# A new table of instruction order and engine choice for a fused cluster-attention and maxout-FFN kernel

## The chip, the cores and the metric

The kernel runs on one core of one Trainium2 chip. The metric is the device time of one execution in microseconds (us); lower is better. The core has five engines that work at the same time and wait for each other through semaphores: TensorE (PE in the profile; its weight loads are PEld), VectorE (DVE), ScalarE (ACT), GpSimd (POOL) and SyncE (SP), which here only issues DMAs.

## The reference

Attention in which a query sees only keys of its own cluster, then a feed-forward layer with a maximum of three products:

```python
# q, k, v: 4 x 8 x 768 x 64; centroids: 8 x 16 x 64; w1, w2, w3: 512 x 768; w_out: 768 x 512
q_assign = argmax(einsum('bhsd,hcd->bhsc', q_n, c_n)); k_assign = the same of k
scores = where(q_assign == k_assign, q @ k.T / sqrt(D), -1e9)
attn = exp(scores - max) / (sum + 1e-9)
x = (attn @ v), heads side by side: 3072 x 512
out = maximum(maximum(x @ w1, x @ w2), x @ w3) @ w_out
```

## The kernel before, in words

The work is cut into 3077 *units*, small closures that each issue one to a few dozen instructions on one engine. Nothing is scheduled at run time: `ORDER` is a written-out list of the 3077 unit numbers, and `Plan.run` calls the units in that order, so each engine's queue holds its own units in the order of the list and runs them strictly in turn. 1104 of the units are *flexible*: they may be issued on VectorE, ScalarE or GpSimd (some on the DMA queue). `HANDS` is a string with one letter for each of them, in the order of unit numbers: V, S, G or Q. Both tables come from a search over the planner's costs (the numbers in us in each `add`); at run time only the tables count.

The stages of the work are interleaved by the table:

- **Preparation of q and k** (`prep`, `mask_rows`, `first_rows`), 16 pairs of heads: load, scale by powers of two, split in a 16-bit high and low part (tile `qk`, lines L380, L378, L382, L804 to L818), cluster scores on TensorE, one-hot rows of the cluster (tile `cl_t`, L527 to L626).
- **Weights** (`weights`, `piece`, `split16`), all in the first 200 us: 24 pieces of 64-bit words are turned into float32 by a cast (tile `top`, L1024 on ScalarE, L1026 on GpSimd) and an integer instruction on VectorE (L1030, from `wd` and `top` to `wf`), then scaled and split (L1041 to L1046). The row maximum of a group is L1070.
- **192 score tiles** (`tile_units`), 48 for each of four batches: four matmuls into a PSUM tile `big` (L1256, L1258); a row maximum on VectorE (L1267, one for each tile, so its count is a ruler for progress); the exponential on ScalarE (L1273); the split in high and low part (`hi`: L378 on ScalarE, L382 on GpSimd or VectorE; `lo`: L1279 on GpSimd or VectorE); then a transposing DMA. 20 tiles of the first batch are transposed on TensorE instead (L1304) and split from PSUM into `pt` (high part L378 or L382, low part L1312 on VectorE). From the second batch on, rows are divided by their sum first (L1293, L1294, then L1321 or L1323, or within L380 and L1332).
- **24 visits** (`visit`), each after six tiles: 36 matmuls with v (L1207). In the first batch the division by the sums follows (L1199 spreads the reciprocals through TensorE, `spread` takes them out of PSUM into `xs` by L378 on ScalarE or L382 on VectorE, L1226 multiplies).
- **Feed-forward** (`ffn`), 8 blocks of 384 tokens: 18 groups of 12 matmuls each (L1413), their evictions with the running maximum (L1427, L380 or L382), a split (L987, L989, L1142), and three output groups of 18 matmuls (L1468) whose results are stored.

The PSUM buffers are few: three `big` and two `one`. A unit that needs a buffer waits for the last user of what lay there before:

```python
        for n in order:
            u = self.units[n]
            for x in u.leases:
                x()
            u.fn(u.hand) if u.pick else u.fn()
...
            for x in u.leases:
                x.left -= 1
                if not x.left:
                    self.places[x.tag].append(x.place)
```

`x()` takes the place that came free first, in the order of the list. So the list also sets which buffer a tile gets, and whose end it waits for.

Of the kernel before, what the change touches and what calls it, by code (L numbers as in the profile page):

```python
# [1534 lines left out]
```

## Time and profile before

| | |
|---|---|
| median of 3 runs | 710.59 us (707.4 to 712.21) |
| profiled execution, its own time | 711.06 us |
| its span, first to last instruction | 709.1 us |
| PE busy | 665.5 us (94%) |
| DVE busy | 599.0 us (84%) |
| ACT busy | 483.6 us (68%) |
| POOL busy | 403.3 us (57%) |
| mean granted TensorE clock | 0.978 |

The times are whole-device times. The span is 2 us shorter than the time of the same execution, since it begins at the first instruction and ends with the last. Busy shares are means over the whole span; the stages differ, so the stretches of the profile are to be read one by one.

### The profile page before, as it was taken

How to read it: one execution, taken by the hardware profiler on the slowest of the kernel's cores; microseconds unless marked ns; L12 is line 12 of the kernel's file. 1: busy time of each engine (PE TensorE's matmuls, PEld its weight loads, DVE VectorE, ACT ScalarE, POOL GpSimd, SP SyncE). 2: the span in 40 equal slices, each digit the busy share in tenths (PEclk: the TensorE clock that was granted, in tenths of full speed). 3: DMA queues.
4: the chain of work that ended last, by engine and by line, in shares of the span. 5: the costliest groups of instructions: out<-in, count | busy, mean ns of one | idle time of the engine just before them, and what ended most of it. 6: DMA issues, size and time to landing. Idle time of an engine off the chain costs nothing. (4 is left out here: it accounts for less than half of the span.)

```text
span 709.1 us, 13176 instructions
## 1 busy us (share of the span) xinstructions
PE 665.5 (94%) x4505; PEld 389.9 (55%) x4505; DVE 599.0 (84%) x1470; ACT 483.6 (68%) x841; POOL 403.3 (57%) x374
## 2 busy tenths in 40 slices
PE   3778778998999999999999999999999999999997
...
PEclk8578999999999999999999999999999999999999
...
GB/s 225 199 216 182 207 210 205 188 174 202 168 196 188 172 126 217 197 185 195 215 156 194 179 189 181 185 196 196 197 194 178 145 164 112 148 158 125 1 1 60
DMA packets 297795, 121.03 MB, mean 171 GB/s; under 512 B 273024, under 2 KB 284160, under 8 KB 297728
## 3 DMA queue, kind: packets, MB, share of 16 engines
...
## 5 line engine op out<-in xcount | busy, mean ns | idle before, releaser
L1267 DVE TENSOR_SCALAR_CACHE_REDUCE big<-big,nsc 128x768 f32<-128x768 f32 x192 | 192.7, 1016 | 11.4 <-PE big L1258 10.8
L1413 PE MATMUL one<-x,w16a 128*128 128x384 f16 x1152 | 197.0, 326 | 0.2
L1279 POOL TENSOR_TENSOR hl<-e,hl 128x768 f16<-128x768 f32 x86 | 144.4, 1682 | 61.1 <-ACT hl L378 34.2
L1413 PEld LDWEIGHTS <-w16a 128*128 128x128 f16 x1152 | 111.5, 98 | 75.7 <-issue 2.9
L1273 ACT ACTIVATE e<-big,nm 128x768 f32<-128x768 f32 x116 | 104.4, 901 | 49.7 <-DVE big L1267 32.3
L1256 PE MATMUL big<-qk 128*128 128x512 f16 (+1 forms) x384 | 96.6, 334 | 12.2 <-ACT e L1273 9.4
L1207 PE MATMUL big<-pt,v 128*64 128x384 f16 x1152 | 101.8, 330 | 2.4 <-ACT e L1273 1.4
L1413 PE MATMUL one<-x,w16b 128*128 128x384 f16 x576 | 98.9, 326 | 1.0 <-DVE worow L1098 1.0
L1258 PE MATMUL big<-qk 96*128 96x512 f16 (+1 forms) x384 | 96.1, 331 | 0.1
L1273 ACT ACTIVATE big<-big,nm 128x768 f32<-128x768 f32 x76 | 66.3, 872 | 43.7 <-DVE big L1267 35.3
L1207 PEld LDWEIGHTS <-v 128*64 128x64 f16 x1152 | 70.0, 111 | 33.2 <-issue 9.8
L1413 PEld LDWEIGHTS <-w16b 128*128 128x128 f16 x576 | 55.7, 98 | 40.1 <-issue 3.4
L1332 DVE SCALAR_TENSOR_TENSOR hl<-big,rs,hl 128x768 f16<-128x768 f32 x72 | 72.7, 1011 | 4.6 <-ACT hl L380 3.6
L380 ACT ACTIVATE hl<-big,rs 128x768 f16<-128x768 f32 x62 | 55.7, 898 | 27.3 <-issue 10.7
L1323 POOL TENSOR_SCALAR e<-e,rs 128x768 f32<-128x768 f32 x37 | 34.0, 919 | 65.9 <-DVE rs L1294 47.1
L1256 PEld LDWEIGHTS <-qk 128*128 128x128 f16 x384 | 35.3, 99 | 43.7 <-issue 22.1
L378 ACT CAST hl<-e 128x768 f16<-128x768 f32 x60 | 49.8, 831 | 5.3 <-POOL e L1323 4.5
L1258 PEld LDWEIGHTS <-qk 96*128 96x128 f16 x384 | 38.2, 100 | 27.1 <-issue 2.6
L818 POOL TENSOR_TENSOR qk<-stage,qk 128x768 f16<-128x768 f32 x26 | 43.8, 1686 | 9.2 <-ACT qk L378 5.5
L1468 PE MATMUL one<-wo,vf_h 128*128 128x512 f16 x216 | 48.3, 379 | 0.5 <-ACT o L380 0.4
L1468 PE MATMUL one<-wo,wf_h 128*128 128x512 f16 x216 | 48.3, 379 | 0.0
L1427 DVE SCALAR_TENSOR_TENSOR wf_h<-one,wf_h 128x384 f32<-128x384 f32 x48 | 26.5, 553 | 20.2 <-PE one L1413 19.6
...
## 6 DMA issues: line engine op xcount, KB each, us to landing
...
```

The lines of the kernel that those rows point to most:

```text
L378: eng.copy(out, x)
L380: eng.activation(out, x, AF.Copy, scale=k)
L818: eng.tensor_tensor(t()[:, AQ, i], x(), t()[:, BQ, i], op=ALU.subtract)
L1207: nc.tensor.matmul(t()[D * i : D * i + D, 0:nb], v()[:, i, kt, a], pts[i % len(pts)]()[:, rows[i], c * QT + kt, :], start=(m == 0), stop=( ...
L1256: nc.tensor.matmul(t()[:, lo:hi], aq[:, qs], ak[:, lo:hi], start=True, stop=False)
L1258: nc.tensor.matmul(t()[:, lo:hi], bq[0:K2, qs], bk[0:K2, lo:hi], start=False, stop=True)
L1267: nc.vector.tensor_scalar(s, s, -SCALE if exact else nscs[:, b, pr : pr + 1], 3.0e38, op0=ALU.mult, op1=ALU.min, accum_out=nm())
L1273: nc.scalar.activation(e(), t()[:, 0:S], AF.Exp, bias=nm(), scale=-1.0, accum_out=r)
L1279: eng.tensor_tensor(hl()[:, 1, :], e(), hl()[:, 0, :], op=ALU.subtract)
L1332: eng.scalar_tensor_tensor(hl()[:, 1, :], e(), r(), hl()[:, 0, :], op0=ALU.mult, op1=ALU.subtract)
L1413: nc.tensor.matmul(t()[:, 0:nb], w16[jt // JA][:, jt % JA, wa, i, ct], x16[b, gi, ct]()[:, xa, 0:nb], start=(m == 0), stop=(m == 3 * CT - 1),)
L1468: nc.tensor.matmul(t()[:, 0:DM], h16(jt)[:, ha, tt * P : (tt + 1) * P], wo16[0][:, jt, wa, :], start=(m == 0), stop=(m == 3 * JT - 1),)
```

## The change: other tables of order and of engines

`ORDER` and `HANDS` are replaced, nothing else. The unit closures, the planner's costs, the buffers and their counts are the same. 279 of the 1104 flexible units get another engine: 59 go from ScalarE to GpSimd, 55 from ScalarE to VectorE, 51 from VectorE to ScalarE, 45 from GpSimd to ScalarE, 36 from VectorE to GpSimd and 33 from GpSimd to VectorE. In instructions VectorE goes from 1280 to 1281, ScalarE from 626 to 608, GpSimd from 379 to 396; TensorE has 8651 and SyncE 374 in both.

```diff
 ORDER = """
-1 0 18 19 51 52 173 445 151 2-5 7 6 54 53 8-15 20 21 30 22-24 39 25 26 40 27 55 28 16 31 33 36 35 56 41 57 63
+1 0 19 18 51 52 151 173 2-5 7 6 53 54 8-15 21 20 30 22-24 39 25 55 26 40 27 56 29 28 41 16 33 31 36 174 57 63
...
 HANDS = """
-VVSSSSSSVVSSSSSSGSGSGGQQGVSSGSGSVGQQGVSSSSGSSGQQGVSGGSVGSSGSSGGSGVSSGSSGSSGSSGVGSGSSGVSGSGGVVSGSGGSGGGGGVSGGSS
+VVSSSSSVVVSSSSSSSSGSGGQQGVSSGGGSSGQQGSVSGGGSSVQQGVSGGGSGSSVSSGGSSVSSGGSGGSGSGSVGSGSSGVSGSSSVSSGSSGSGGSSGVVSGGS
...
```

**First place, TensorE some 50 us into the program.** L1304 transposes a finished tile, L412 spreads a scale of the weights, L1256 and L1258 are the next score tile, L1207 is the first product with v. Before:

```order
L1304 MATMUL big<-ident,e 128x128 x6
L412 LDWEIGHTS sc_m
L412 MATMUL one<-ident,sc_m 128x128
L1256 LDWEIGHTS qk
L1256 MATMUL big<-qk 128x512
L1256 LDWEIGHTS qk
L1256 MATMUL big<-qk 128x256
L1258 LDWEIGHTS qk
L1258 MATMUL big<-qk 128x512
L1258 LDWEIGHTS qk
L1258 MATMUL big<-qk 128x256
L1207 LDWEIGHTS v_326
```

The same place after:

```order
L412 LDWEIGHTS sc_m
L412 MATMUL one<-ident,sc_m 128x128
L1256 LDWEIGHTS qk
L1256 MATMUL big<-qk 128x512
L1256 LDWEIGHTS qk
L1256 MATMUL big<-qk 128x256
L1258 LDWEIGHTS qk
L1258 MATMUL big<-qk 128x512
L1258 LDWEIGHTS qk
L1258 MATMUL big<-qk 128x256
L1304 MATMUL big<-ident,e 128x128 x6
L1207 LDWEIGHTS v_412
```

The score tile now stands ahead of the transposes of an older tile, where it stood behind them.

**Second place, VectorE some 31 to 38 us into the program.** `hl`, `qk` and `v` are high parts, L543 and L555 belong to the one-hot rows, L733 is an absolute maximum of q and k. Before:

```order
L1267 TENSOR_SCALAR big,nm<-big,nsc 128x768
L382 TENSOR_SCALAR v_397<-vf 128x12x64
L757 SCALAR_TENSOR_TENSOR nsc<-q_p 128x1
L382 TENSOR_SCALAR hl<-e 128x768
L543 TENSOR_TENSOR cl_t_313<-rank,cl_m_314 128x768
L1267 TENSOR_SCALAR big,nm<-big,nsc 128x768
L1312 TENSOR_TENSOR pt<-big,pt 128x768
L1030 SCALAR_TENSOR_TENSOR wf<-wd,top 128x512
L382 TENSOR_SCALAR qk<-stage_261 128x768
L555 TENSOR_SCALAR cl_t_313<-one,ksel 128x768
L1312 TENSOR_TENSOR pt<-big,pt 128x768
L1267 TENSOR_SCALAR big,nm<-big,nsc 128x768
```

The same place after:

```order
L1030 SCALAR_TENSOR_TENSOR wf<-wd,top 128x512
L543 TENSOR_TENSOR cl_t_314<-rank,cl_m_315 128x768
L762 TENSOR_REDUCE q_s<-q_r 128x1
L1267 TENSOR_SCALAR big,nm<-big,nsc 128x768
L626 STREAM_TRANSPOSE cl_t_239<-onehot_99 128x768
L1267 TENSOR_SCALAR big,nm<-big,nsc 128x768
L1312 TENSOR_TENSOR pt<-big,pt 128x768
L733 TENSOR_REDUCE q_m_391<-stage_373 128x1
L382 TENSOR_SCALAR pt<-big 128x768
L1267 TENSOR_SCALAR big,nm<-big,nsc 128x768
L1312 TENSOR_TENSOR pt<-big,pt 128x768
```

Four eviction-sized steps have left VectorE here (`v`, `hl`, `qk`, L555, all to ScalarE), and two have come to it (L733 and a high part `pt` from PSUM, both from ScalarE).

**Third place, VectorE some 80 us into the program**, between two score tiles of the first batch. Before:

```order
L415 TENSOR_REDUCE wcol<-one 128x1
L416 RECIPROCAL sc_s<-wcol 128x1
L1030 SCALAR_TENSOR_TENSOR wf<-wd,top 128x512
L1267 TENSOR_SCALAR big,nm<-big,nsc 128x768
L1043 TENSOR_SCALAR wf<-wf,sc_s 128x512
L1030 SCALAR_TENSOR_TENSOR wf<-wd,top 128x512
L1312 TENSOR_TENSOR pt<-big,pt 128x768 x2
```

The same place after:

```order
L1267 TENSOR_SCALAR big,nm<-big,nsc 128x768
L1030 SCALAR_TENSOR_TENSOR wf<-wd,top 128x512
L1043 TENSOR_SCALAR wf<-wf,sc_s 128x512
L1267 TENSOR_SCALAR big,nm<-big,nsc 128x768
L1030 SCALAR_TENSOR_TENSOR wf<-wd,top 128x512
L1312 TENSOR_TENSOR pt<-big,pt 128x768
L382 TENSOR_SCALAR xs<-one 128x384
L1312 TENSOR_TENSOR pt<-big,pt 128x768
```

A `spread` (`xs` from PSUM) has come to VectorE from ScalarE; there are four such of eight in the new table and none in the old one.

## Rows read from the trace of the kernel before

**Rows 1.** The page, parts 1 and 2: busy time of each engine with its share and count, and the span in 40 slices of 17.7 us (tenths busy; PEclk is the granted TensorE clock in tenths).

```profile
span 709.1 us, 13176 instructions
PE 665.5 (94%) x4505; PEld 389.9 (55%) x4505; DVE 599.0 (84%) x1470; ACT 483.6 (68%) x841; POOL 403.3 (57%) x374
PE   3778778998999999999999999999999999999997
PEclk8578999999999999999999999999999999999999
```

**Rows 2.** Busy time of each engine in stretches of the span: the stretch, its length, then PE, PEld, DVE, ACT, POOL busy us (instructions), the granted clock, the DMA share and GB/s.

```profile
20.00:60.00 40.00, 33.30 (x187) 22.32 (x187) 36.48 (x76) 35.21 (x59) 29.49 (x21) 0.71 0.85 197
60.00:200.00 140.00, 121.71 (x912) 74.54 (x910) 136.37 (x311) 125.31 (x231) 111.93 (x100) 1.00 0.82 193
200.00:300.00 100.00, 99.45 (x677) 58.20 (x676) 87.03 (x225) 66.06 (x112) 57.87 (x49) 1.00 0.90 180
300.00:400.00 100.00, 99.74 (x691) 57.30 (x689) 93.17 (x244) 72.72 (x125) 65.99 (x55) 1.00 0.94 188
400.00:640.00 240.00, 239.31 (x1626) 139.00 (x1625) 209.52 (x532) 163.50 (x284) 128.40 (x111) 1.00 0.88 172
640.00:710.00 70.00, 65.20 (x399) 35.55 (x397) 20.95 (x39) 6.84 (x12) 2.76 (x4) 0.99 0.18 45
```

**Rows 3.** The end of the chain that ended last: start us, us, what.

```profile
...
655.29 3.05 PE big L1207 x36
658.34 35.21 PE one L1413 x216
693.54 11.67 PE one L1468 x54
```

**Rows 4.** Who waited for whom from 20 to 200 us, for TensorE and for VectorE: the waiting engine, tile and line, what ended the wait, us in total, times, the longest.

```profile
PE big L1256 <- ACT e L1273: 9.4, 12, 1.4
PE big L1304 <- ACT e L1273: 3.7, 5, 1.3
...
DVE big L1267 <- PE big L1258: 1.6, 4, 1.0
DVE xs L1226 <- PE big L1207: 1.5, 2, 1.3
```

**Rows 5.** VectorE in order of time at two places: some 53 to 59 us, and at 199.5 us the 57th row maximum. Columns: start us, us, engine, line, operation, operands, count, and in brackets the idle time before it and what ended it.

```profile
53.96 1.02 DVE L1267 TENSOR_SCALAR_CACHE_REDUCE big<-big,nsc 128x768 f32<-128x768 f32 x1 [0.99 <-PE big L1258]
58.66 0.56 DVE L1226 TENSOR_TENSOR xs<-big,xs 128x384 f32<-128x384 f32 x1 [1.28 <-PE big L1207]
199.51 1.01 DVE L1267 TENSOR_SCALAR_CACHE_REDUCE big<-big,nsc 128x768 f32<-128x768 f32 x1
```

**Rows 6.** VectorE's groups by line and shape: line, operation, out<-in with shapes, count, busy us, mean ns of one, idle us before.

```profile
L1312 DVE TENSOR_TENSOR pt<-big,pt 128x768 f16<-128x768 f32 x20 | 18.9, 950 | 1.2 <-ACT pt L378 0.9
L1279 DVE TENSOR_TENSOR hl<-e,hl 128x768 f16<-128x768 f32 x10 | 10.6, 1057 | 0.3
L382 DVE TENSOR_SCALAR hl<-big,rs 128x768 f16<-128x768 f32 x10 | 10.1, 1014 | 0.2
L382 DVE TENSOR_SCALAR hl<-e 128x768 f16<-128x768 f32 x13 | 7.2, 552 | 0.6 <-ACT e L1321 0.6
L382 DVE TENSOR_SCALAR wf_h<-one 128x384 f32<-128x384 f32 x13 | 7.2, 552 | 3.3 <-PE one L1413 3.2
L382 DVE TENSOR_SCALAR o<-one,so 128x512 f32<-128x512 f32 x8 | 6.0, 748 | 9.6 <-PE one L1468 9.6
L818 DVE TENSOR_TENSOR qk<-stage,qk 128x768 f16<-128x768 f32 x4 | 5.4, 1342 | 0.0
L382 DVE TENSOR_SCALAR qk<-stage 128x768 f16<-128x768 f32 x4 | 2.5, 628 | 0.0
L1323 DVE TENSOR_SCALAR e<-e,rs 128x768 f32<-128x768 f32 x4 | 3.3, 821 | 0.0
L989 DVE TENSOR_SCALAR vf_h<-vf_h 128x384 f16<-128x384 f32 x8 | 2.8, 354 | 0.0
L904 DVE TENSOR_TENSOR v<-stage,v 128x768 f16<-128x768 f32 x2 | 1.9, 951 | 0.0
L589 DVE TENSOR_TENSOR cl_t<-cl_t,cl_m 128x384 f32<-128x384 f32 x2 | 1.7, 859 | 0.0
```

**Rows 7.** TensorE from 49 to 59 us in order of time, the columns of rows 5.

```profile
49.35 0.48 PE L1256 MATMUL big<-qk 128*128 128x512 f16 x2 [1.13 <-ACT e L1273]
50.61 1.54 PE L1304 MATMUL big<-ident,e 128*128 128x128 f32 x6 [0.45 <-ACT e L1273]
52.44 0.84 PE L1256 MATMUL big<-qk 128*128 128x512 f16 x2
53.85 4.74 PE L1207 MATMUL big<-pt,v 128*64 128x384 f16 x36
```

**Rows 8.** The integer instruction L1030 on VectorE: its row by line (duration ns min/median/max, first and last start), one instance, and one of GpSimd at that place (start us, us).

```profile
L1030 DVE SCALAR_TENSOR_TENSOR wf<-wd,top x24: 672/692/1945, 19.8 to 156.3; 128x512 int32<-128x512 int32 x24
...
43.47 1.95 DVE L1030 SCALAR_TENSOR_TENSOR wf<-wd,top 128x512 int32<-128x512 int32 x1
...
43.22 1.64 POOL L1279 TENSOR_TENSOR hl<-e,hl 128x768 f16<-128x768 f32 x1
```

**Rows 9.** The group of the same line by shape: count, busy us, mean ns.

```profile
L1030 DVE SCALAR_TENSOR_TENSOR wf<-wd,top 128x512 int32<-128x512 int32 x24 | 19.2, 799 | 0.3 <-POOL w16a L1046 0.2 <-ACT top L1024 0.2
```

More of the change, by code (lines that the diff above doesn't have):

```diff
@@ L77 @@
-1507 1479 1470 1497 2699 1498 1508 1492 1483 1509 1460 2700 2702-2704 1510 1493 1461 1499 1511 1494 1462 1484
[7 rows of a table removed]
-1602 1618 1610 1603 1625 2729 601 633 1626 2730 1611 605-607 2733 1633 1642 2735 2731 1619 1627 1628 1634 1643
[8 rows of a table removed]
-1695 1723 1733 691 712 1741 2762 2763 619 1734 713 714 620 684 1742 2764 2768 1735-1737 1724 1725 695 621 1738
[12 rows of a table removed]
-1869 1870 2812 2946 1904 1839 1896 1871 1905 1872 1897 1873 1840 2814 1898-1900 1882 1891 1874 1912 2817 1913
-1914 2818 1906 1901 1929 2819 2821 1920 2815 1915 1916 1930 1917 1918 1907 1931-1933 1908 2816 2820 2822 1921
[10 rows of a table removed]
@@ L119 @@
-2071 2078 2859 2079 817 2091 2861 792 2092 818 819 2100 2080 820-822 2072 2860 793 2093 859 2862 2053 856 2064
[11 rows of a table removed]
-2900 893 2230 848 2231 2225 2237 2902 2245 918 913 914 2212-2214 877 2198 936 2215 2226 2905 2253 2907 2238
[11 rows of a table removed]
-945 2407 2396 3007 2367 2388 2950 2377 2368 2397 2408 2400-2402 3067 2409 2410 2952 2411 2415 2423 2424 2416
-2425 2954 2443 2412 2403 2417 2426 2404 2418 2419 2427 2413 2428 2420 2444 2445 2955 2378 2435 2379 2429 2421
-2380 2430 2446 2447 2436 2448 2437 2452 2957 2959 2469 2405 2422 2431 2414 2453 2438-2441 2470 2958 2471 2454
[9 rows of a table removed]
@@ L155 @@
-3010 3015 2596 3017 3019 3018 3020 3021 3025 3022-3024 3026 3027 3029 3028 3033 3030 3031 3034 3032 3035 3037
-3036 3041 3038-3040 3042 3043 3045 3044 3046-3049 3051 3050 3052 3053 3057 3054 3058 3055 3056 3059 3061 3060
-3062-3064 3068 3071 3069 3070 3016 3074 3072 3073 3075 3076
+1 0 19 18 51 52 151 173 2-5 7 6 53 54 8-15 21 20 30 22-24 39 25 55 26 40 27 56 29 28 41 16 33 31 36 174 57 63
[15 rows of a table added]
+1137 1149 1119 1143 1138 1150 229 1144 230-232 1120 1139 1151 1140 1116 245 248 1121 1141 1145 246 1146 247
[14 rows of a table added]
@@ new lines @@
+388 1273 1282 1252 492 1283 2635 1284 1288 389-393 494 495 2645 434 1248 421 432 525 431 465 1274 2637 439
[3 rows of a table added]
+1307 472 473 1314 2649 1315 1316 1256 502-504 1320 505 1326 1335 1321 1294 1322 1327 474 1336 475 2651 536
+1292 1308 1317 477-479 476 538 1328 1323 1337 1343 1295 1324 1338 1339 1329 506 532 1344 1340 1345 1296 533
+507 534 1297 1341 1298 1299 509 535 570 2650 1325 510 480 508 1355 1363 1346 512 1330 1356 1357 2652 1300
+1331-1333 1372 2657 2654 1373 1358 1359 1364 1360 2658 1374 537 513 514 1361 539 540 1347 1348 1365 2655 1349
[5 rows of a table added]
@@ new lines @@
+2765 1427 561 1412 1371 555 1388 556 628 1396 1405 583 2681 2683 2680 1428 2682 562-564 1429 1413 1414 1422
+488 2684 565 1430 1415 2685 2689 1443 1423 1424 489 2686 2766 1435 1444 2687 1431 1436 1445 1437 1438 1432
+1446 2691 1451 1406 1416 569 566-568 1425 1433 1447 1439 2688 1440 1452 1448 2690 1453 1407 1449 546 2692 1454
+1408 1455 1456 1441 1457 2693 1471 1463 1488 2697 1472 1464 1458 2694 577 1473 1465 1450 1442 1459 1474 1466
+1467 1475 2695 1476-1478 1489 1468 2698 1490 1480 2701 1505 1469 1506 1491 1492 1481 1507 1493 2696 2656 1470
@@ new lines @@
+1479 2653 584 1497 2699 1498 1460 1508 2700 1509 1482 1499 2702 2703 1510 2704 1483-1485 1500 1494 1511 1501
[5 rows of a table added]
+1591-1593 1597 599 1584 595 2723 2724 596 1585 1598 1605 2725 1613 1594 2827 1599 1606 1607 1614 597 1586 602
[8 rows of a table added]
+652 1702 1714 690 2757 1721 1676 2759 653-655 1691 1709 1710 2758 1715 1692 656 657 2755 1693 1716 658 1722
[18 rows of a table added]
+1953-1955 1967 1959 1968 1969 1960 1961 1974 1983 2834 1956 766 2776 1962 1963 1975 1984 1976 1985 1977 1970
+1971 1978 2832 1986-1988 2835 2947 1972 1989 1979 1964 1980 1946 1991 2003 1947 1948 1992 2004 2011 2837 2839
[5 rows of a table added]
@@ new lines @@
+788 2068-2070 789 2085 2856 2086 2061 2062 2074 2857 2099 817 2075 790 2063 2076 2077 2858 2078 818 791 2079
[9 rows of a table added]
+880 2191 2201 2187 2192 809 881 810 2202 2203 882 905 883-886 2193 2194 2204 2195 2188 906 2205 2162 907 2207
[8 rows of a table added]
+2315 941 2308 942 946 2316 2289 2297 2309 2317 947 943 855 944 2927 948 2217 2310-2312 2218 2313 2929 2931
+2327 2335 2270 2336 2328 3065 2318 2319 2304 2928 2305 2930 2329 2932 2320 899 2337 2321 2322 2330-2332 2271
+2272 2338 2333 2339 2340 2314 2306 2323 2893 2937 2933 2352 2344 2369 2934 2353 2935 2345 2341 900 2354 2346
@@ new lines @@
+2938 2355 2370 2347 3066 3005 2348 2356 2936 2342 2349 2371 2350 2357 2358 2343 2351 2334 2939 2361 2941 2389
+2372 2362 2940 2390 2942 2373 2359 2363 2391 2374 2324 2381 2392 3006 2382 2943 2325 2375 2383-2385 2393 2364
[3 rows of a table added]
+2436 2437 2452 2957 2469 2959 2405 2414 2422 2431 2453 2438-2440 2958 2454 2448 2441 2470 2471 2455 2472 2960
+2456 2460 2965 2961 2473 2457 2458 2461 2474 2462 2449 2962 2463 2464 2475 2432 2477 2489 2967 2442 2459 2476
+2963 2465 2433 2966 2434 2497 2969 2478 2490 2964 2450 2968 2466 2467 2498 2491 2479 2499 2492 2970 2971 2506
@@ L158 @@
+2973 2514 2975 2493 2480 2500 2501 2468 2451 2494 2502 2972 2503 2974 2507 2495 2481-2483 2504 2515 2484 2531
[6 rows of a table added]
+3019 3018 3020 3021 3025 3022 3023 3026 3024 3027 3029 3028 3033 3030-3032 3034 3035 3037 3036 3041 3038 3039
+3042 3040 3043 3045 3044 3046-3049 3051 3050 3052 3053 3057 3054 3058 3055 3056 3059 3061 3060 3062-3064 3068
+3071 3069 3070 3074 3072 3073 3016 3075 3076
 """
 HANDS = """
-VVSSSSSSVVSSSSSSGSGSGGQQGVSSGSGSVGQQGVSSSSGSSGQQGVSGGSVGSSGSSGGSGVSSGSSGSSGSSGVGSGSSGVSGSGGVVSGSGGSGGGGGVSGGSS
@@ L162 @@
-GSSVSGSVSSGSSGSSGSGSVSSGGGGSSGGSSGSSSGSSGGSSGGGSSGGGSGSVSGGSSGQQGGVGSVSSSSGGGGQQGGVGSGSSVGGSSVQQGGVGSGSSGVGSSG
-QQVGVSGGSVGSGGSGQQVGVSGGVSSSGSVGQQGGVSSGVSGGGSSGQQGVVSSGSSSVGGGVQQGGVSSGSSGSGGSVQQVGVGSGSVSSGVSGQQVGVSSVSSGSGG
-SGQQGGVSSGSSGGGGSVQQGGVGSGSVGSGGSSGSGGSVGSSGSVGSSGSVGSSGSGGSSGSSGSSGSSVSSGSSGSSGSSGSSGSSGSSVSSGSSGSSGSSGSVSGSG
-GSVSVSVSGSVSGSVGSVSSGSVGGGSVSSGVSVSSGSVVSGSVGSGVSVSSGSVSVGSVGGVVSVGGGSVGSGSVGSGSSVGGGSVGSGSVSSGSVVGSVSVGGGSVSS
-GSSVGSGSVSGGVVSSGSSVSSGSVSGGSVGGGSSVVSGVVGVGSVSSGSSVGSGSVSSGSVGSGVSVGSGSVGSGVVSGGSSVVVGSVGGVSVGGGSVVGVGVVGSGSV
@@ L167 @@
-SGGVSVGGGSVGSGSVGSGVSVSGGSVSSGSVSSVSSVSGGSVSSGSVGVGSSVGSGSVGSGSVSGGSSVVSGSVGSGSVSGGSSVGGGSVSSGSVSSVSVVGVGSVGSG
-SVSSGSSVGSGSVSVGSVGSVSVVGGGSVGVGVVGSGVSVSSGSVGSGSVSVGVVVSGGSVSSGSVSGVSSVVVGSVVSGVVVSGSVVSVVVVGGSVVGGSVSVVVGVSV
-VSGSVVSGSVVVGVVVGGVVVVVSVSSVVVGSVVSGSVVSGSVVSGSVVVGSVVSGSSSVVVGGVVVSGVVVSGSVVSGSVVGGVVVGVSSVVVVSGSVVGGSVVGGVVV
-VGSVVSGSVVVVVSSVVVGGSVVGGSVVVGSVVGVSVVVVVVVGGSSSSVVSVSVVVVVVVSGSVVVVVVVVGSVVGVVVVVVVSVVVVSGVVVSVVVVGVSVVVVSVVV
-VVSS
+VVSSSSSVVVSSSSSSSSGSGGQQGVSSGGGSSGQQGSVSGGGSSVQQGVSGGGSGSSVSSGGSSVSSGGSGGSGSGSVGSGSSGVSGSSSVSSGSSGSGGSSGVVSGGS
```

14 lines of the change are left out of this document (10 added, 4 removed), and 211 rows, old and new, of the table ORDER.

## The prediction

> **What bounds the kernel now.** I read the page first, then the stretches, then the waits inside the stretch that loses time. The page shows TensorE busy for 665.5 of 709.1 us [rows 1], so the shares name TensorE as the bound; but a share is a mean over unlike stages. The stretches tell them apart [rows 2]. From 200 to 640 us TensorE is busy for 99.45 of 100, 99.74 of 100 and 239.31 of 240 us: it loses 1.5 us in 440. In the last stretch it works without a break until about 705 us, and the end of the chain is TensorE alone, 35.21 us of L1413 and then 11.67 us of L1468 [rows 2, 3]. So nothing can be gained after 200 us; the matmuls there are the same in either order. From 20 to 200 us TensorE is idle for 6.7 + 18.3 = 25.0 us, and up to 60 us it has a mean granted clock of 0.71, a mixture of its two levels, 1.2 and 2.4 GHz.
>
> Who makes it wait there? By the view of waits it is the exponential on ScalarE that frees a `big` buffer (9.4 us) or delivers the tile that is to be transposed (3.7 us) [rows 4]. But the exponential itself follows the row maximum on VectorE, and VectorE is busy for 36.48 of 40 and 136.37 of 140 us, more than ScalarE's 35.21 and 125.31 [rows 2]. VectorE idles for only 3.5 + 3.6 = 7.1 us in these 180, of which two kinds of wait for TensorE make 3.1 [rows 4]. I therefore take VectorE's queue as what paces the first 200 us: TensorE gets ahead of it only as its buffers allow. The time is then VectorE's work up to about 200 us, plus its few waits, plus the TensorE work left from there.
>
> **The change part by part.** The TensorE stream keeps its instructions, and its units move by a few places at most. What counts is what VectorE has to do before it reaches the same tile.
>
> *VectorE's load up to 200 us.* The 57th row maximum starts at 199.51 us [rows 5]. Counted in the two orders, 370 units stand ahead of it before and 371 after, but other ones. More: 3 of L1312 at 0.950 = 2.85; 3 low parts (two L818, one L904) at L904's 0.951 = 2.85; 9 of half a microsecond (4 spreads `xs`, 2 high parts `v`, 2 low parts of 384 columns, one scaling of weights), at 0.552 by the row of `wf_h` from PSUM. Fewer: 3 of L1279 at 1.057 = 3.17; one `o` at 0.748; one `qk` at 0.628; 2 of L989 at 0.354 = 0.71; 7 half-microsecond steps (2 `hl`, 2 evictions, one `v`, one scaling, one take of one-hot rows) at the same 0.552 [rows 6]. The sum is 2.85 + 2.85 + 2 x 0.552 - 3.17 - 0.75 - 0.63 - 0.71 = +1.5 us. With the two L818 at their own mean of 1.342 instead it is +2.3. The own mean holds a slow instance or two among four, so I take the middle, **+1.9 us**. The second and third places show its kind: VectorE gives up one-source steps and takes work that reads PSUM.
>
> *A wait that goes.* At 53.96 us VectorE waits 0.99 us for a score tile, since TensorE first had to wait at 50.61 us for the exponential before the transposes [rows 5, 7]. At the first place the tile now stands ahead of these transposes, and in the new order the L1312 that frees its buffer has less VectorE work ahead of it. I count **-1.0 us**; the bounds are -1.0 and 0, since the transposes come later instead and the product with v waits for them either way. The wait of 1.28 us at 58.66 us for that product (4.74 us, in the stretch of mean clock 0.71) [rows 5, 7] I leave as it is.
>
> *ScalarE and GpSimd.* ScalarE loses 18 instructions, GpSimd gains 17. Up to 200 us neither is the fullest engine [rows 2], so I cost this at nothing; VectorE's 97% of 60 to 200 us hides it. If it did not, the price would be in GpSimd's grip on VectorE, a rival below.
>
> *After 200 us.* Over the whole kernel VectorE's load grows too: 6 more `hl` from PSUM and 3 more `pt` high parts at 1.014, 3 of L589 at 0.859 and 3 of L1323 at 0.821 make 14.2 us; 4 of L1279, 4 of `qk`, 3 of L989 (net) and one `o` less make 8.6 us [rows 6]; the rest about cancels. That is some +5.6 us, 3.7 of it after 200 us. VectorE has 13.0 us of idle time from 200 to 300 and 6.8 from 300 to 400 [rows 2], while TensorE is fed from a backlog. I count **0**; bounds 0 and +1.8, half of it, should the denser stretch be entered late.
>
> *The end.* TensorE's last 50 us have the same units in both orders: 0.
>
> The sum: 711.06 + 1.9 - 1.0 = 711.96 us for the profiled execution (its span 709.1 and 2.0 around it). That execution lies 0.47 above the median of the runs, so as a median **711.5 us**. Each term has its sign, but a measurement here cannot tell 1% (7.1 us) from no change; this forecast is "no change".
>
> **A rule weighed.** One integer instruction, L1030, takes 672 to 1945 ns for the same shape, with a median of 692 [rows 8]. The long one at 43.47 us lies beside GpSimd's L1279, which started 0.25 us earlier and ended at 44.86; L1030 ends 0.56 us after that [rows 8]. The Trainium skill, "SBUF — State Buffer", section "Who interferes with whom", says that an instruction of VectorE with two inputs in SBUF contends with a GpSimd instruction that reads SBUF, and that the one that comes second fully blocks until the first is done. The trace agrees at this instance. It speaks against a change that gives GpSimd more to do: by that rule the sum is the second rival's, by the rows as they stand it is the forecast's.
>
> **The rivals.**
> *TensorE's waits are the pace, and the new order removes them.* For it: TensorE idles for 25.0 us from 20 to 200 us, and it waits for single buffers, which the order hands out. Against it: VectorE has only 7.1 us of idle time to be saved there, and does 1.9 us more. If all of that idle time went, the time would be 711.06 - 7.1 + 1.9 = 705.9, as a median 705.4. If the first product with v, 4.74 us, also ran as the 36 matmuls at the end do, in 3.05 [rows 3, 7], it would be 703.7.
>
> *GpSimd holds VectorE up more often.* L1030 costs 24 x (0.799 - 0.672) = 3.0 us more than 24 of its shortest instances [rows 8, 9]. The new table has GpSimd work at other moments, and VectorE has more low parts that read two SBUF tiles as well. Should the collisions double, with the load at its upper bound and the 1.0 us wait not gained, the sum is 711.06 + 2.3 + 3.0 = 716.4; with the 1.8 us of the later stretch 718.2, as a median 717.7. It makes the kernel slower than before from the point at which VectorE loses more than the 1.0 us that the wait gives back; for over 1% all of these have to come together. Against it: collisions can as well fall; all of L1030's gone would give 3.0 us back.
>
> *The change does not do what it says.* The counts on TensorE and SyncE are the same, so nothing is hidden in it; no chance.
>
> **How the numbers follow.** Forecast (709 to 714.5): 0.58. TensorE's waits removed: 0.25, of which 0.10 lies below 703.5, where fewer collisions have to help (705.4 - 3.0 = 702.4). Collisions: 0.17, of which 0.10 lies above 717.7 and 0.08 above 718.5. The range reaches from 703.5, next to the 703.7 of the one rival, to 718.5, next to the 718.2 of the other: 0.82 of the chance. Against the median of 710.59 the bounds of 1% are 703.5 and 717.7, so: faster 0.10, same 0.80, slower 0.10.
>
> **What would show it.** In the profile of the changed kernel: VectorE busy over 96% from 60 to 200 us, and TensorE idle for 23 to 27 us from 20 to 200 us; no wait of VectorE for TensorE of about 1 us near 53 us; the 57th row maximum at 199 to 202 us; TensorE at over 99% from 200 to 640 us; VectorE's total busy time some 5 us higher, ScalarE's lower. The forecast is wrong if VectorE's share up to 200 us falls while the tiles come earlier (then it was not the pace), if L1030's mean goes well above 0.8 us, or if TensorE shows new waits of several microseconds after 200 us.

## The result, and the profile after

The changed kernel takes 717.25 us (median of 6 runs, 715.7 to 717.93), the kernel before, run beside it, 711.53 us (6 runs, 707.4 to 713.11). The ratio is 1.0083, with a 95% interval of 1.0055 to 1.0111: slower, by 0.8%. The forecast was 711.5 us with a range of 703.5 to 718.5.

The page after, its span and busy times, against [rows 1]:

```profile
span 714.2 us, 13172 instructions
PE 669.5 (94%) x4505; PEld 390.9 (55%) x4505; DVE 604.7 (85%) x1471; ACT 469.4 (66%) x824; POOL 417.9 (59%) x391
```

The stretches after, columns as in [rows 2]:

```profile
20.00:60.00 40.00, 30.44 (x179) 21.50 (x180) 35.89 (x76) 34.09 (x58) 28.06 (x22) 0.87 0.71 182
60.00:200.00 140.00, 125.84 (x918) 74.99 (x918) 135.82 (x315) 126.07 (x229) 111.61 (x96) 0.96 0.90 195
200.00:300.00 100.00, 98.17 (x670) 57.90 (x669) 89.03 (x229) 61.05 (x113) 57.27 (x48) 1.00 0.89 177
300.00:400.00 100.00, 97.77 (x668) 55.71 (x668) 94.03 (x240) 69.75 (x119) 64.91 (x56) 1.00 0.95 187
400.00:640.00 240.00, 238.67 (x1625) 138.65 (x1622) 211.00 (x527) 154.28 (x271) 141.25 (x125) 1.00 0.88 170
```

Up to 200 us little has changed: TensorE idles for 9.6 + 14.2 = 23.7 us, where it was 25.0. From 200 to 640 us it idles for 1.8 + 2.2 + 1.3 = 5.4 us, where it was 1.5. The loss lies where the prediction counted nothing. Who it waits for there, after (columns as in [rows 4]):

```profile
PE big L1256 <- ACT e L1273: 1.2, 3, 0.5
PE big L1258 <- DMA qk<-cl_t: 1.1, 1, 1.1
PE one L1413 <- ACT vf_h L380: 0.6, 1, 0.6
PE big L1256 <- DVE hl L1332: 0.6, 1, 0.6
PE one L749 <- DVE vf_h L1427: 0.4, 1, 0.4
PE one L749 <- DVE q_m L743: 0.4, 1, 0.4
...
```

and the same view before, whole:

```profile
PE big L1207 <- ACT e L1273: 0.5, 2, 0.3
PE big L1256 <- DVE hl L1332: 0.3, 1, 0.3
PE big L1256 <- DVE x L1179: 0.3, 1, 0.3
```

No single wait is large. The 1.1 us are for the mask rows of one score tile (unit 1417), which a DMA brings; most of the others are for a buffer of `big` or `one` that came free late. To place them I compare starts of the same TensorE unit in both traces, at places where the same units stand ahead of it in both orders. The lateness of the new kernel is -0.23 us at unit 2669 (211.90 us before, 211.66 after). Further on, by the time in the trace before, it is +1.05 at 302 us, +3.37 at 331, +4.43 at 468, +5.61 at 525, and +5.14 at the start of the last 35 us of L1413, which [rows 3] had at 658.34:

```profile
663.48 35.21 PE one L1413 x216
```

So 5.4 us are lost behind 212 us, 2.3 of them between 302 and 331 us. On VectorE there, in order of time (columns as in [rows 5]):

```profile
305.36 1.02 DVE L1267 TENSOR_SCALAR_CACHE_REDUCE big<-big,nsc 128x768 f32<-128x768 f32 x1
...
306.29 1.78 DVE L615 TENSOR_SCALAR onehot<-cl_t,ksel 128x768 f16<-128x768 f16 x1
...
308.06 0.54 DVE L1427 SCALAR_TENSOR_TENSOR vf_h<-one,vf_h 128x384 f32<-128x384 f32 x1
...
466.65 1.57 DVE L761 TENSOR_TENSOR q_r<-q_r,hsel 128x2 f32<-128x2 f32 x1
```

GpSimd at the same two places:

```profile
306.21 1.64 POOL L1279 TENSOR_TENSOR hl<-e,hl 128x768 f16<-128x768 f32 x1
...
466.56 1.64 POOL L1279 TENSOR_TENSOR hl<-e,hl 128x768 f16<-128x768 f32 x1
```

and what TensorE does meanwhile:

```profile
308.65 0.22 PE L749 MATMUL one<-ident,q_m 128*128 128x128 bf16 x1 [0.44 <-DVE vf_h L1427]
...
310.08 2.11 PE L1413 MATMUL one<-x,w16a 128*128 128x384 f16 x12 [0.56 <-ACT vf_h L380]
```

L615 began 0.08 us after GpSimd's L1279 and ended 0.22 us after it; L761, on 128 x 2 numbers, began 0.09 us after another and ended 0.02 after it. Before, the same L615 (unit 612) took 0.40 us, the same L761 (unit 820) 0.15. The eviction L1427 queued behind L615 is what the first wait of TensorE names. A held instruction is shown as *busy*, not as waiting.

Such instructions can be counted. I call a VectorE instruction held if it takes over 0.1 us more than the shortest of its line and shape in the same trace, and that excess its hold. From 212 to 640 us there are 9 before, with 4.8 us of hold, and 15 after, with 10.8 us; each of them begins while a GpSimd instruction runs and ends with it or after it. The groups show it by their means; before (columns as in [rows 6]):

```profile
L615 DVE TENSOR_SCALAR onehot<-cl_t,ksel 128x768 f16<-128x768 f16 x14 | 6.4, 454 | 0.1
L757 DVE SCALAR_TENSOR_TENSOR nsc<-q_p 128x1 f32<-128x1 f32 x16 | 3.2, 199 | 0.0
L761 DVE TENSOR_TENSOR q_r<-q_r,hsel 128x2 f32<-128x2 f32 x16 | 2.6, 161 | 0.1
```

and after, with the group of [rows 9] and one that reads PSUM:

```profile
L615 DVE TENSOR_SCALAR onehot<-cl_t,ksel 128x768 f16<-128x768 f16 x14 | 7.8, 555 | 0.2
L757 DVE SCALAR_TENSOR_TENSOR nsc<-q_p 128x1 f32<-128x1 f32 x16 | 4.0, 252 | 0.0
L761 DVE TENSOR_TENSOR q_r<-q_r,hsel 128x2 f32<-128x2 f32 x16 | 5.6, 348 | 0.1
L1030 DVE SCALAR_TENSOR_TENSOR wf<-wd,top 128x512 int32<-128x512 int32 x24 | 18.3, 763 | 0.9 <-ACT top L1024 0.6 <-POOL top L1026 0.4
L1332 DVE SCALAR_TENSOR_TENSOR hl<-big,rs,hl 128x768 f16<-128x768 f32 x72 | 72.6, 1009 | 4.9 <-ACT hl L380 3.4 <-POOL hl L382 1.0 <-issue 0.2
```

Three groups of unchanged count take 1.4 + 0.8 + 3.0 = 5.2 us more, where VectorE's busy time grew by 5.7 in all. The groups whose count changed take some 0.5 us more together. L1030, on which the prediction priced the collisions, takes less. L1332, which reads one of its two tiles from PSUM, has the same mean as before (72.7 us, 1011 ns), and none of its 72 takes over 1.02 us in either trace.

Two marks of the prediction, VectorE after:

```profile
53.42 1.02 DVE L1267 TENSOR_SCALAR_CACHE_REDUCE big<-big,nsc 128x768 f32<-128x768 f32 x1
...
199.07 1.01 DVE L1267 TENSOR_SCALAR_CACHE_REDUCE big<-big,nsc 128x768 f32<-128x768 f32 x1
```

The wait of 0.99 us of [rows 5] is gone, and the 57th row maximum starts 0.44 us earlier, not 0.9 later.

### The profile page after: what moved, and what is told of

Read it like the earlier page. It is cut to its first block, busy times and chain, and to the rows that moved or that the text cites. A ratio compares the mean times of both kernels' runs of the same rounds, so it can differ in the third digit from the quotient of the medians.

```text
span 714.2 us, 13172 instructions
## 1 busy us (share of the span) xinstructions
PE 669.5 (94%) x4505; PEld 390.9 (55%) x4505; DVE 604.7 (85%) x1471; ACT 469.4 (66%) x824; POOL 417.9 (59%) x391
## 5 line engine op out<-in xcount | busy, mean ns | idle before, releaser
L1267 DVE TENSOR_SCALAR_CACHE_REDUCE big<-big,nsc 128x768 f32<-128x768 f32 x192 | 192.5, 1017 | 10.8 <-PE big L1258 7.4
L1413 PE MATMUL one<-x,w16a 128*128 128x384 f16 x1152 | 197.7, 326 | 0.7 <-ACT vf_h L380 0.6
L1279 POOL TENSOR_TENSOR hl<-e,hl 128x768 f16<-128x768 f32 x90 | 150.0, 1668 | 66.6 <-ACT hl L378 42.5
L1413 PEld LDWEIGHTS <-w16a 128*128 128x128 f16 x1152 | 111.7, 98 | 76.7 <-issue 3.3
L1256 PE MATMUL big<-qk 128*128 128x512 f16 (+1 forms) x384 | 97.7, 337 | 13.9 <-DVE pt L1312 5.7
L1207 PE MATMUL big<-pt,v 128*64 128x384 f16 x1152 | 101.9, 331 | 1.6 <-ACT e L1273 1.1
L1413 PE MATMUL one<-x,w16b 128*128 128x384 f16 x576 | 99.4, 326 | 0.1
L1258 PE MATMUL big<-qk 96*128 96x512 f16 (+1 forms) x384 | 97.5, 335 | 1.1 <-DMA qk<-cl_t 1.1
L1207 PEld LDWEIGHTS <-v 128*64 128x64 f16 x1152 | 69.5, 111 | 32.3 <-issue 9.8
L1332 DVE SCALAR_TENSOR_TENSOR hl<-big,rs,hl 128x768 f16<-128x768 f32 x72 | 72.6, 1009 | 4.9 <-ACT hl L380 3.4
L1413 PEld LDWEIGHTS <-w16b 128*128 128x128 f16 x576 | 55.7, 98 | 38.5 <-issue 1.9
L380 ACT ACTIVATE hl<-big,rs 128x768 f16<-128x768 f32 x56 | 50.2, 899 | 20.5 <-issue 8.3
L1256 PEld LDWEIGHTS <-qk 128*128 128x128 f16 x384 | 35.0, 100 | 47.8 <-issue 18.7
L1258 PEld LDWEIGHTS <-qk 96*128 96x128 f16 x384 | 38.5, 101 | 28.7 <-issue 3.0
L1323 POOL TENSOR_SCALAR e<-e,rs 128x768 f32<-128x768 f32 x34 | 31.9, 938 | 36.7 <-DVE rs L1294 18.9
L378 ACT CAST hl<-e 128x768 f16<-128x768 f32 x51 | 42.3, 829 | 11.9 <-POOL e L1323 7.5
L382 POOL TENSOR_SCALAR hl<-e 128x768 f16<-128x768 f32 x32 | 26.9, 842 | 37.7 <-ACT e L1321 19.0
L818 POOL TENSOR_TENSOR qk<-stage,qk 128x768 f16<-128x768 f32 x25 | 41.6, 1670 | 5.6 <-ACT qk L378 5.2
```

The costliest lines, as they stand in the source:

```text
L378: eng.copy(out, x)
L380: eng.activation(out, x, AF.Copy, scale=k)
L818: eng.tensor_tensor(t()[:, AQ, i], x(), t()[:, BQ, i], op=ALU.subtract)
L1207: nc.tensor.matmul(t()[D * i : D * i + D, 0:nb], v()[:, i, kt, a], pts[i % len(pts)]()[:, rows[i], c * QT + kt, :], start=(m == 0), stop=( ...
L1256: nc.tensor.matmul(t()[:, lo:hi], aq[:, qs], ak[:, lo:hi], start=True, stop=False)
L1258: nc.tensor.matmul(t()[:, lo:hi], bq[0:K2, qs], bk[0:K2, lo:hi], start=False, stop=True)
```

## The experiments

**The halves.** At the 1052nd unit of both lists (some 212 us) the same units stand ahead, so a list can be cut there and go on with the other; each unit keeps the engine that its table gives it. The new start with the old rest is the old list with its first 1052 numbers in the new order, the other half the reverse:

```diff
 ORDER = """
-1 0 18 19 51 52 173 445 151 2-5 7 6 54 53 8-15 20 21 30 22-24 39 25 26 40 27 55 28 16 31 33 36 35 56 41 57 63
+1 0 19 18 51 52 151 173 2-5 7 6 53 54 8-15 21 20 30 22-24 39 25 55 26 40 27 56 29 28 41 16 33 31 36 174 57 63
...
```

> Order and engines of the new tables for the first 1052 units of the list (some 212 us), of the old ones for the rest; at that cut the same units stand ahead in both lists. Theory A (the loss is made after 212 us, by what the new tables do there): at the cut TensorE is as far as before (0.2 us earlier in the trace of the changed kernel), the rest runs as before, so 711 us, ratio 0.997 to 1.002, and TensorE idles for under 2 us from 212 to 640 us. Theory B (the new start leaves fewer finished tiles behind it, and TensorE pays for that later): 715 to 717 us, ratio 1.005 to 1.009, with waits of several us after 212 us.

> The other half: old tables for the first 1052 units, new ones for the rest. Theory A: the loss comes whole, 5.4 us (the 5.1 at the end and the 0.2 that the new start had gained): 716 to 717 us, ratio 1.006 to 1.010, and TensorE's waits stand at the same units as in the changed kernel (near 219, 303 to 330, 390 and 475 to 500 us). Theory B: 711 us, ratio 0.998 to 1.002.

> The changed kernel once more, unaltered, for a second trace. If its late waits come from the tables, TensorE waits at the same units again (score tiles or groups near 219, 303 to 330, 390 and 475 to 500 us), each within 0.5 us of its first length, and the ratio is 1.006 to 1.011. If they come from chance in the transfers, other units wait, and the sum differs by more than 2 us.

Measured: new start, old rest 712.67 us, ratio 1.0008 (0.9982 to 1.0035). Old start, new rest 718.09 us, ratio 1.0078 (1.0043 to 1.0113). The changed kernel again 716.04 us, ratio 1.0050 (1.0025 to 1.0074), just under the 1.006 expected. Theory A holds: the slowdown goes with the new rest. How late TensorE is against the trace of before, at the cut (unit 2669) and at the start of its last but one L1413 group (unit 3061), the difference, which is what is lost behind the cut, and VectorE's hold from 212 to 640 us (4.8 before):

| kernel | at the cut | at the end | lost behind the cut | VectorE's hold |
|---|---|---|---|---|
| changed | -0.23 | +5.14 | 5.4 | 10.8 |
| changed, second trace | -1.65 | +4.07 | 5.7 | 10.9 |
| old start, new rest | +2.30 | +10.41 | 8.1 | 9.9 |
| new start, old rest | +0.40 | +1.63 | 1.2 | 5.1 |
| new middle (below) | -1.97 | -0.86 | 1.1 | 4.8 |
| changed, units moved (below) | -1.92 | +1.13 | 3.1 | 6.3 |
| new middle, three edits (below) | +0.15 | +2.28 | 2.1 | 4.5 |
| new middle, two edits (below) | -4.83 | -3.21 | 1.6 | 6.9 |
| new middle, three other edits (below) | -2.66 | -2.38 | 0.3 | 5.0 |

The second trace of the changed kernel has the same waits at the same units (634, 2743, 1696, 1704, 1866, 862, 2173), each within 0.1 us of its first length; only the tile 1417 waits 1.3 in place of 1.1. Behind the cut this program repeats itself, and the loss belongs to the tables. So does the hold: 10 to 11 us with the new rest as it stands, about 5 in the first two kernels with the old one. Ahead of the cut the program does not repeat itself: the same tables reach the cut up to 2.3 us apart. The old start with the new rest loses 3.7 of its 8.1 us by 231 us, where the changed kernel loses 1.0 (the tile 1417 waits 2.2 us for its mask rows there), and then 4.4, as the changed kernel does (4.4). The 1.1 and 1.2 of the kernels with the old rest come from the seam: two waits just behind it that neither whole list has.

```profile
PE one L412 <- DVE wf_h L1427: 1.0, 2, 0.5
```

is their row in the view of TensorE's waits from 200 to 640 us of the new start with the old rest.

**Order without its engines.** The two tables crossed:

```diff
 HANDS = """
-VVSSSSSVVVSSSSSSSSGSGGQQGVSSGGGSSGQQGSVSGGGSSVQQGVSGGGSGSSVSSGGSSVSSGGSGGSGSGSVGSGSSGVSGSSSVSSGSSGSGGSSGVVSGGS
+VVSSSSSSVVSSSSSSGSGSGGQQGVSSGSGSVGQQGVSSSSGSSGQQGVSGGSVGSSGSSGGSGVSSGSSGSSGSSGVGSGSSGVSGSGGVVSGSGGSGGGGGVSGGSS
...
```

> The new order with the old choice of engines for all 1104 flexible units. Theory E (the order makes the loss): 716 to 718 us, ratio 1.006 to 1.010. Theory F (the engine choice makes it): 711 us, ratio 0.998 to 1.002. Theory G (order and engines were fitted to each other, and neither half works with the other's partner): more TensorE waits than in either kernel, over 10 us from 212 to 640 us, ratio above 1.012.

> The old order with the new choice of engines. Theory E: 711 us, ratio 0.998 to 1.002. Theory F: 716 to 718 us, ratio 1.006 to 1.010. Theory G: more TensorE waits than in either kernel, ratio above 1.012.

Measured: 788.47 us, ratio 1.1056 (1.1017 to 1.1096), and 793.86 us, ratio 1.1148 (1.1102 to 1.1195). Theory G holds: neither half works with the other's partner. The new order with the old engines, from 60 to 200 us:

```profile
60.00:200.00 140.00, 110.30 (x750) 65.77 (x750) 123.99 (x245) 106.82 (x199) 95.20 (x83) 0.90 0.73 159
```

VectorE is busy for 124 of 140 us, where either whole kernel has 136. No engine is full: each is busy for less of the stretch than in either whole kernel. The tables of engines differ in 279 letters of 1104 only, and yet either mixture costs over ten times what the new pair costs against the old.

**Held instructions, or a full engine?** Seven units of the changed kernel moved by a few places. Two of the places, as pieces of the list:

```diff
-2737 2741 612 1645 2738 1646 613 1647 2742 1640 2739 2740 1632 1641 1667 634 1659 2743 1653 635
+2737 2741 1645 2738 1646 1647 2742 1640 2739 2740 1632 1641 1667 634 1659 2743 1653 612 613 635
...
-1352 553 1417 2673 2675
+1352 553 2673 1417 2675
```

> The changed kernel with seven units moved by a few places, engines and work as they are. On VectorE: the one-hot unit 612 (L615, 1.78 us at 306.29, begun 0.08 us after a GpSimd L1279) and the transpose 613 after it go behind four short units; 682 (L761, 1.59 us at 317.78, begun 0.07 us after a GpSimd L818) goes behind two units that read PSUM; 820 (L761, 1.57 us at 466.65, begun 0.09 us after a GpSimd L1279) and 821 behind two such; 822 (L757, 1.03 us at 473.44, inside a GpSimd L818) ahead of the transpose before it. On TensorE: score tile 1417, which waits 1.14 us for its mask rows at 219, goes behind the next feed-forward group. Theory H (VectorE held up by GpSimd in single instructions makes the late waits): the four instructions take 0.2 to 0.5 us each, TensorE's waits at units 634, 2743, 1696, 1704 and 862 (0.4, 0.6, 0.2, 0.5 and 0.4 us) and 1417 (1.1 us) go, and TensorE loses 2 to 3 us from 212 us to the end, against the old kernel, where it lost 5.4 and 5.7: 713 to 714 us, ratio 1.002 to 1.005. Rival I (VectorE and ScalarE are simply too full there; the held-up instructions are incidental): the waits move to other units, TensorE loses 4.5 to 6 us, ratio 1.005 to 1.009.

Measured: 713.01 us, ratio 1.0007 (0.9983 to 1.0031), against 1.0083 and 1.0050 of the changed kernel. The four instructions take 0.45, 0.20, 0.15 and 0.14 us:

```profile
306.06 0.45 DVE L615 TENSOR_SCALAR onehot<-cl_t,ksel 128x768 f16<-128x768 f16 x1
...
317.08 0.20 DVE L761 TENSOR_TENSOR q_r<-q_r,hsel 128x2 f32<-128x2 f32 x1
...
468.35 0.14 DVE L757 SCALAR_TENSOR_TENSOR nsc<-q_p 128x1 f32<-128x1 f32 x1
```

TensorE's waits at 634, 2743, 1696, 1704 and 862 are gone; one of 0.35 us at 309.66 us is new. VectorE's hold behind the cut falls from 10.8 to 6.3 us. From 300 to 400 us TensorE is busy for 99.18 us, where it was 97.77 after and 99.74 before:

```profile
300.00:400.00 100.00, 99.18 (x685) 57.64 (x684) 93.64 (x244) 68.67 (x118) 66.65 (x58) 1.00 0.98 190
```

Theory H holds, with a loss of 3.1 us just above the 2 to 3 expected; the time lies at the lower end of its 713 to 714, and the ratio below that, since the old kernel beside it took 712.14, not 710.59. An edit both ends the hold and puts evictions ahead of the moved instruction, and the run by itself does not tell the two apart. At the first place the trace of the changed kernel does: there the eviction L1427 (308.06) starts as the held L615 ends (308.07), and TensorE starts as L1427 ends (308.60). One of the five places failed: the score tile 1417 no longer waits, but the group after it does, almost as long, for an eviction on ScalarE that stands behind that tile's exponential:

```profile
223.08 1.14 PE L1413 MATMUL one<-x,w16a 128*128 128x384 f16 x6 [1.05 <-ACT wf_h L380]
```

Its wait has changed its name only. What is left of the loss, 3.1 us, is this one and small waits, none over 0.6 us; no run here takes these apart.

**Is there a gain ahead of 212 us?** In the changed kernel's trace VectorE is 4.1 us late at the 30th row maximum (some 104 us) and 0.4 us early at the 57th (some 199 us). The new list for that stretch alone, between its 467th and 1052nd unit:

```diff
 ORDER = """
 1 0 18 19 51 52 173 445 151 2-5 7 6 54 53 8-15 20 21 30 22-24 39 25 26 40 27 55 28 16 31 33 36 35 56 41 57 63
...
-1122 248 251 233 1155 1169 1181 1156 234 403 235 402 1123 404 236 1157 1161 242 237 1158 239 1124 249 2599
+1122 248 251 233 1155 1136 1152 1169 249 1123 403 402 1153
...
```

> Old tables up to the 467th unit of the list (some 104 us), new ones from there to the 1052nd (212 us), old ones to the end. In the trace of the changed kernel VectorE is 4.3 us late at 104 us and level again at 187 us, and its instructions that run longer than others of their shape lose 6.7 us from 100 to 200 us before and 2.2 after. Theory C (these hold-ups belong to the order, and VectorE paces this stretch): 4 us are gained, 707 us, ratio 0.992 to 0.996. Rival D (the hold-ups follow from how far GpSimd and VectorE happen to stand to each other, and return elsewhere): 711 us, ratio 0.998 to 1.002.

Measured: 707.38 us, ratio 0.9942 (0.9915 to 0.9969). Theory C's time came out (the one trace shows less of the gain, 0.9 us at the end). The traces agree with its reason: from 104 to 212 us VectorE's hold is 6.7 us before and 7.2 in the old start with the new rest, both of them with the old tables there, and 1.1 in the new middle and 0.8 in the changed kernel. Just ahead of this stretch, still under the old tables, L1030 of unit 247 took 2.06 us at 103.33 (0.69 before).

**Three more edits there.** They went by theory H, on a cut at the 1103rd unit:

```diff
-230 1139 1140 1151 1141 1145 1120 1146 231 1142 232 1092 1116 245 1121 246 1147 247
+230 1139 1140 1151 1141 1145 1120 1146 245 246 247 231 1142 232 1092 1116 1121 1147
...
-1273 1282 1252 492 1283 2635 1284 1288 389 390 391 392 393 494
+1273 389 390 391 392 393 1282 1252 492 1283 2635 1284 1288 494
```

> Old tables up to the 467th unit, new ones from there to the 1103rd (some 224 us, not 212), old ones to the end, with the three edits that theory H asks for in that stretch: L1030 of unit 247 (2.06 us beside a GpSimd L1279 at 103.33 us) goes ahead of three short units, with the load and the cast that feed it; the five weight scalars 389 to 393 (0.54 and 1.22 us for the last two, beside GpSimd at 168 us) go ahead of a row maximum; score tile 1417 goes behind the next feed-forward group. Theory H: up to 1.4 and 1.3 us less on VectorE ahead of 170 us, and some 1 us less lost from 212 to 224 us, where the cut at 212 left waits of 0.53 and 0.44 us: 704 to 706 us, ratio 0.988 to 0.992. Rival (the stretch up to 200 us is set by TensorE's buffers or by chance in the transfers, so that single held-up instructions don't count): 707 to 708 us, ratio 0.993 to 0.996.

Measured: 712.56 us, ratio 0.9994 (0.9969 to 1.0019): worse than without them, and outside what either theory had expected. The first edit did what it should (L1030 took 0.69 us). The five weight scalars ran into other GpSimd instructions at their new place, and the two row maxima behind them came 2.4 us later than in the new middle. On VectorE and on GpSimd:

```profile
164.61 0.77 DVE L1123 TENSOR_SCALAR r_o<-worow,sc_s 128x6 f32<-128x6 f32 x1
165.41 1.56 DVE L1124 TENSOR_TENSOR r_o<-r_o,wcol 128x6 f32<-128x6 f32 x1
```

```profile
164.20 1.15 POOL L1046 TENSOR_TENSOR wo<-wf,wo 128x512 f16<-128x512 f32 x1
165.31 1.63 POOL L1279 TENSOR_TENSOR hl<-e,hl 128x768 f16<-128x768 f32 x1
```

The longer new list brought the wait behind tile 1417 along, 1.20 us at 233 us.

**Two edits.** The first of the three stays, and one at the seam is new:

```diff
-2667 2669 1382 1383 2668 2670 1397 574 484
+2667 2669 1382 2668 2670 1383 1397 574 484
```

> The kernel with the new middle (old tables up to unit 467 of the list, new ones to 1052, old ones to the end) with two edits. L1030 of unit 247 goes ahead of three short units with its load and cast, as in the run before, whose trace showed 0.70 us for it in place of 2.06. Behind the cut the evictions 2668 and 2670 go ahead of unit 1383, a small step that waits on VectorE until 212.47 us for an exponential while the evictions are ready at 210.1 and 212.0 us; TensorE's waits of 0.53 and 0.44 us at 213 us are for these. If single held-up or badly placed instructions count in full where a queue paces: TensorE gains 1 to 1.5 us at 104 to 126 us and 1.0 us at 213 us against the kernel with the new middle, and the median falls by about 2 us: 705 us, ratio 0.989 to 0.993. If not: no change against it, 707 us, ratio 0.993 to 0.996.

Measured: 707.22 us, ratio 0.9924 (0.9898 to 0.9950). The waits at 213 us are gone, and at the cut TensorE is 2.9 us ahead of the new middle. The median is not ahead (707.38 there), and the interval of the ratio covers both outcomes that were expected. Behind the cut TensorE lost 1.5 us at once, at a place where no number of the list had changed. VectorE, GpSimd and TensorE there:

```profile
474.40 0.95 DVE L952 TENSOR_REDUCE vmax<-stage 128x1 f32<-128x768 f32 x1 [0.56 <-DMA stage<-in_v_dram]
...
476.28 1.92 DVE L580 TENSOR_TENSOR cl_t<-cl_t 128x384 f32<-128x384 f32 x1
```

```profile
476.14 1.64 POOL L818 TENSOR_TENSOR qk<-stage,qk 128x768 f16<-128x768 f32 x1 [0.19 <-ACT qk L378]
```

```profile
478.72 0.48 PE L1413 MATMUL one<-x,w16b 128*128 128x384 f16 x2 [0.94 <-DVE rs L1293]
```

The same two instructions in the new middle without the edits, on VectorE and on GpSimd:

```profile
479.72 0.56 DVE L580 TENSOR_TENSOR cl_t<-cl_t 128x384 f32<-128x384 f32 x1
```

```profile
480.00 1.78 POOL L818 TENSOR_TENSOR qk<-stage,qk 128x768 f16<-128x768 f32 x1 [0.19 <-ACT qk L378]
```

With the same tables L580 began 0.28 us ahead of GpSimd in the one and 0.14 us behind it in the other, since VectorE had waited 0.56 us for a load just before. The hold cost VectorE 1.36 us, and TensorE lost 1.5; since the 0.56 us for the load stand ahead of the same eviction, how much of the 1.5 is the hold's stays open. (The wait is put down to L1293; the buffer's last user is the eviction L1427 just ahead of that, which starts at 478.12 behind L580.) The last run takes the waiting load out of the way:

```diff
-802 833 834 2874 2139
+833 834 2874 802 2139
```

> The kernel of the run before (new middle, two edits) with one more: on VectorE the column maximum 802 (L952, waits for a load of v) goes behind three units, the transpose 833 (L577), the sum 834 (L580) and the eviction 2874. In the run before, 802 waited 0.56 us for its load, 834 therefore began at 476.28, 0.14 us after GpSimd's L818 (unit 873, 476.14 to 477.78), and took 1.92 us; with the same tables in the kernel with the new middle, 834 began 0.28 us ahead of 873 and took 0.56. Theory H (one held instruction costs TensorE its excess where nothing is spare): 834 takes 0.55 us, TensorE's wait of 0.94 us at 478.72 is gone and it loses under 0.5 us from 212 us to the end in place of 1.7; 705.5 us, ratio 0.989 to 0.993. Rival (that wait belongs to the eviction's late place behind the load, not to the hold): it comes back at another unit, 707 us, ratio 0.991 to 0.995, TensorE loses 1.5 us or more.

Measured: 707.84 us, ratio 0.9948 (0.9922 to 0.9974). L580 takes 0.56 us, the wait is gone, and 0.3 us are lost behind the cut, as theory H has it. It is no proof against its rival: the edit takes the load's wait from the eviction together with the hold, and TensorE came to this place 1.9 us later than in the run before. The time and ratio that theory H expected did not come out. The whole time did not fall; this kernel reached the cut 2.2 us later than the run before it, at places that were not edited. The three kernels with the new middle up to the 1052nd unit, at 0.992 to 0.995, are all faster than before, and these runs can't tell them apart.

## Why the prediction was right and wrong

The forecast was no change, and the slowdown of 0.8% lies inside the 1% that was counted as none; the time lies 5.8 us above the forecast, in the range's upper part. That a measurement here cannot tell 1% from no change was wrong: the interval from 1.0055 to 1.0111 does.

**What bounds the kernel: half right.** Up to 200 us VectorE stays the fullest engine (97.0% from 60 to 200) and TensorE's idle time is the 23 to 27 us foretold. That TensorE is the bound after 200 us was right as well, though its share from 200 to 640 us is 98.8%, not over 99. The conclusion that nothing changes there failed.

**The term that failed: "After 200 us", 0 with bounds 0 and +1.8.** It was 5.4 and 5.7 us in two traces. Some 2.3 to 2.7 of these went when held instructions were moved, about 1 is the wait at the score tile 1417, for which the sum has no term, and about 2 are small waits whose cause stays open. Two steps in the term were wrong. First, TensorE "is fed from a backlog": with three `big` and two `one` buffers there is hardly one. VectorE's 13.0 and 6.8 idle microseconds of [rows 2] are sums over hundreds of instructions; a hold just ahead of an eviction reaches TensorE nearly whole or in half, whatever is idle 5 us later (L615's 1.38 us of hold made TensorE 1.28 us later). A TensorE that loses 1.5 us in 440 is the state that is easiest to spoil: a change of order can hardly win there and can lose at every place. Second, VectorE's growth of +5.6 us was foretold by counts and measured as 5.7, by chance: the groups whose count changed take only some 0.5 us more, since some of their old instances had been held too (L589 at 859 ns, now 554), and three groups of unchanged count take 5.2 us more.

**The load of +1.9 and the wait of -1.0.** The wait went as foretold. The load can't be judged: the 57th row maximum came 0.44 us earlier, but traces of the same tables reach the cut up to 2.3 us apart, more than the whole term. In its list the 3 of L1312 are in truth 3 high parts `pt` (L382, 952 ns in the trace after); L1312 has 20 in both kernels, and the sum stands. A term below that spread should have been called unmeasurable instead of being worked out to a tenth.

**The rival that came out.** GpSimd holding VectorE up was named, with 717.7 us, and given 0.17. The mechanism was right, the place and the rows were wrong, and that its 717.7 us lies 0.5 us from the result is luck. It was priced on L1030, whose last instance starts at 156.3 us [rows 8] and which got cheaper (19.2 to 18.3 us); it had the wait of 1.0 us not gained, but that went; and it had 1.8 us after 200 us, where 5.4 were lost. Small instructions after 200 us decided. The row that would have shown this stood in the trace of before, by line (columns as in the first of [rows 8]): none of the 16 L761 was held for long *yet*. Before and after:

```profile
L761 DVE TENSOR_TENSOR q_r<-q_r,hsel x16: 142/152/292, 11.0 to 513.7; 128x2 f32<-128x2 f32 x16
...
L761 DVE TENSOR_TENSOR q_r<-q_r,hsel x16: 140/158/1586, 11.1 to 519.5; 128x2 f32<-128x2 f32 x16
```

For these instructions the risk in a new order was one-sided. From 104 to 212 us it went the other way: there the old order held VectorE for 6.7 us and the new one for 0.8.

**The rule weighed.** In the traces before and after, 73 VectorE instructions that read two tiles of SBUF start while a GpSimd instruction runs, and 72 of them end after it, also where there are two numbers for each partition: 1.57 us beside a GpSimd L1279 of 1.64. Of L1332, with one tile in PSUM, 147 start so, and 76 of them end before the GpSimd instruction does. The Trainium skill, "SBUF — State Buffer", section "Who interferes with whom", says just this ("Issue order, not op shape, decides who blocks"), and that an instruction with at most one input from SBUF, outside the two-port modes, stays clear. L1332 agrees. Of L615, which has one tile as input and was held for 1.38 us, the page's two-port modes would be the reason; no run here shows its mode.

**The first rival**, TensorE's waits up to 200 us removed: 1.3 us of 25 went. The new middle shows that more can be had there, some 0.6%, only not by these tables as a whole.
